# All row-tile pairs of w_sp·z2 and the product with w_out by seven block products for eight

## The chip, the cores and the metric

The kernel runs on one core of a Trainium2 chip. TensorE (PE) multiplies, VectorE (DVE), ScalarE (ACT) and GpSimd (POOL) do the element-wise work, and all transfers between DRAM and SBUF are issued in order by SyncE (SP) into one queue. The metric is the device time of one execution in microseconds, lower is better; from run to run it differs by a few tenths of a per cent.

## The reference

One block: a linear-attention half and a gMLP half, both with adaLN modulation. S = 2048 tokens, D = 512, F = 1376, Fh = F/2 = 688, float32.

```python
h = layernorm(x) * (1 + ca) + sa
x = x + ga * linear_attention(h, wqkv, wo)      # 32 heads
h = layernorm(x) * (1 + cb) + sb
z = gelu(h @ w_in)                              # (S, 1376)
z1, z2 = z[:, :688], layernorm(z[:, 688:])
g = w_sp @ z2 + b_sp[:, None]                   # (S, S) times (S, 688)
out = x + gb * ((z1 * g) @ w_out)               # (S, 688) times (688, 512)
```

## The kernel before

Tokens are cut into 16 tiles of 128 (NT = 16). Float32 accuracy comes from splitting every operand into a part rounded for fast products ("hi") and the rest ("lo"): one product is three matmuls, hi·hi, hi·lo and lo·hi (`mm3`). The hi part is an ACT copy, the lo part a DVE (at places POOL) subtraction, so that every operand costs work there before PE can use it.

The order of the work is written out by hand. `ORDER` is a list of words for the first phases (qkv, attention, x1, z), `ORDER3` for the late phase; a word is two letters and arguments (`pr1,0,3` calls `prod(1, 0, 3)`), `OPS` says which function. Each engine gets its instructions in this order, and waits for tiles with semaphores. `SLOTS` says which buffer of a pool each tile takes.

The late phase. z2 tiles (`zs` pool, hi and lo, 688 columns as two halves LO and HI of 344) stay in SBUF; their normalized values are also written to DRAM (`zd`). w_sp is loaded in pieces `raw_wsp` (512 KB). g is made in pairs of row tiles, p = 0 to 7:

- Pair 0 (row tiles 0 and 1) by plain products, `pp` (`plain`, PSUM tile Pq): 4 × 2 × 2 × 4 calls of three matmuls of 344 columns, 192 in all, with w_sp's hi and lo from `aH`, `aL`; `ce` (`q_end`) adds the bias and multiplies with z1.
- Pairs 1 to 7 by seven block products for eight, `pr` (`prod`, PSUM tiles P): the row-tile pair and a pair of source tiles form a 2×2 block matrix, the two halves of z2's columns the other side. That needs sums and differences of w_sp's blocks (`ss`, four per pair and half; hi `fh`, lo `fl` on DVE or `fg` on POOL) and of z2's (`ts` reads a pair of z2 tiles back from `zd` as e and o, `td` makes differences by four DVE subtractions, `th` and `tl` the hi and lo parts). 7 × 2 × 4 × 3 = 168 matmuls a pair, 1176 in all. `cs`, `cd` add the products up out of PSUM.

Then u = z1·g per tile (`um`), 16-bit planes of it (`up`), a transposing DMA (`ux`), a merge (`ug`), and u, now transposed, is parked in DRAM (`uq`, tile `ud`, 384 KB) and later fetched back (`ur`); `uh`, `ul` make its hi and lo parts (`ut`). `wm` (`wout_mm`) multiplies a token tile with w_out: 17 matmuls of 512 columns into tile `pout`; the last tile in two halves of 256 columns. `ot` (`out_store`) adds x1 and writes the output.

Buffers: early pools (`ws`: wk, wv and then w_in's halves; `ta`; `tb`) are closed before the late phase, and late pools (`u`, `z1`, `c1` to `c3`, `tq`) lie on their space, each tile waiting for the tiles under it.

Of the kernel before, what the change touches and what calls it, by code (L numbers as in the profile page):

```python
# [19 lines left out]
ND = 4  # L20
DIGITS = "0123456789abcdefghijklmnopqrstuvwxyz"
# [5 lines left out]
def block_kernel(ctx: ExitStack, tc: tile.TileContext, x, x_t, w_qkv, w_o, w_in, w_sp, b_sp, w_out,  # L27
# [3 lines left out]
    def pool(name, bufs, space=None, stack=None):  # L31
        if space is None:
# [6 lines left out]
    sizes2 = {"ws": ([P, 5504], 2), "ta": ([P, 512], 6), "tb": ([P, 768], 7)}  # L39
    sizes3 = {"u": ([P, 768], 2), "z1": ([P, 688], 1), "c1": ([P, 344], 1), "c2": ([P, 344], 1), "c3": ([P, 344], 1),  # L40
              "tq": ([P, 688], 24)}
# [134 lines left out]
    def silu():  # L176
        e0 = sm([P, KC], "e0")
# [167 lines left out]
    wk = sb("ws", [P, 2, KC, D], F32R, "wk")  # L345
# [338 lines left out]

    def z2_hi(t):
# [85 lines left out]
    def hx_lo(t):  # L771
# [12 lines left out]
        "lh": load_half, "aH": a_hi, "aL": a_lo, "aG": lambda t, k: a_lo(t, k, nc.gpsimd),  # L784
# [15 lines left out]
        gm5 tl10 bl7 kh6 q45 s19 k27 km8 qm7 k47 q26 ks6 lx13 k18 th13 s110 kl6 kh7 ks7 q46 q21 k28 km9 q17  # L800
# [385 lines left out]
```

## Time and profile before

| | us |
|---|---|
| median of 3 runs (range) | 617.22 (616.88 to 618.18) |
| profiled execution | 616.95 |
| its span on the core | 615.0 |
| PE busy / weight loads | 608.7 / 555.6 |
| DVE busy | 464.2 |
| ACT busy | 362.2 |
| POOL busy | 212.2 |
| granted PE clock | 1.00 |
| DMA | 105.74 MB, mean 172 GB/s |

The span is what the hardware profiler records from the first instruction to the last; the execution's own time has some 2 us around it. A row of the timeline has start, duration, engine, line, operation and tiles. A row of the groups has line, engine, operation, output<-input, shape and count, then busy us, mean ns of one, and the idle time just ahead of these instructions with what ended it. Line numbers are those of the kernel before; names have their running numbers left out.

### The profile page before, as it was taken

Reading aid. Unit: us, or ns where it says so; the run is one execution under the profiler, and the core shown is the slowest. Engines: PE = TensorE matmul, PEld = TensorE weight load, DVE = VectorE, ACT = ScalarE, POOL = GpSimd, SP = SyncE. Lnnn points to the kernel's source line nnn. Section 1 sums busy time; section 2 is a strip of 40 time slices with the busy share of each in tenths; the row PEclk is TensorE's granted clock in tenths of the full one; section 3 lists DMA queues with packets and bytes.
Section 4 is the critical chain, followed back from the end, with each engine's and each line's share of the span. In section 5 each row is a group of like instructions: output and inputs, shape, how many; then the busy total and the mean of one; then the engine's idle time right before and its main releaser. Section 6 shows DMA issues by size and latency. Waiting matters only on the chain.

```text
span 615.0 us, 9440 instructions
## 1 busy us (share of the span) xinstructions
PE 608.7 (99%) x3359; PEld 555.6 (90%) x3359; DVE 464.2 (75%) x873; ACT 362.2 (59%) x619; POOL 212.2 (34%) x180
## 2 busy tenths in 40 slices
PE   8999999999999999999999999999999999999997
PEld 6778888888889999999999999999999999998786
DVE  2889987987898787879866999966568667765643
ACT  2786765767556656565775166566565656644450
POOL 0852346536966665365320103022112121200000
PEclk9999999999999999999999999999999999999999
DMA  8352331441344866468918645564564866589973
GB/s 303 126 179 98 122 118 44 147 165 40 87 109 120 185 147 192 136 170 260 274 59 326 270 148 169 126 195 101 192 208 129 229 140 175 196 243 284 311 239 113
DMA packets 91022, 105.74 MB, mean 172 GB/s; under 512 B 57088, under 2 KB 57600, under 8 KB 90976
## 3 DMA queue, kind: packets, MB, share of 16 engines
q1 hardware_dynamic: 90976, 105.15, 56.9%
q8 instruction: 26, 0.43, 0.3%
q14 instruction: 20, 0.16, 0.1%
HBM read 66.07 MB, written 25.95 MB: 150 GB/s over the span
## 4 chain that ended last, share of the span: by engine, by line
PE 84%; DVE 7%; ACT 3%; DMA 3%; POOL 1%; issue 1%; SPq 1%; ACTq 0%; DVEq 0%; POOLq 0%
PE P L944 30%; PE z L654 13%; PE Pq L944 5%; PE z L860 2%; PE g L112 2%; PE g L110 2%; PE pout L112 2%; PE g L111 2%; PE pout L110 2%; PE pout L111 2%; PE qp L111 2%; PE qp L110 2%; PE qp L112 2%; PE kp L110 2%; PE kp L111 2%; PE kp L112 2%
## 5 line engine op out<-in xcount | busy, mean ns | idle before, releaser
L944 PE MATMUL P<-z,f 128*128 128x344 f32 x672 | 109.8, 320 | 0.0
L654 PE MATMUL z<-win,ht 128*128 128x344 f32 x672 | 107.9, 320 | 0.2 <-ACT z L659 0.2
L654 PEld LDWEIGHTS z<-win,ht 128*128 128x128 f32 x672 | 106.4, 188 | 1.3 <-ACT z L659 0.5
L944 PEld LDWEIGHTS P<-z,f 128*128 128x128 f32 x672 | 106.6, 188 | 0.0
L934 POOL TENSOR_TENSOR f<-raw_wsp,f 128x512 fp32r<-128x512 f32 x28 | 39.6, 1423 | 172.7 <-ACT f L931 150.2
L254 POOL TENSOR_TENSOR mv<-ve,mhalf 128x1 f32<-128x1 f32 x48 | 35.2, 736 | 68.3 <-DVE nm L387 34.4
L931 ACT ACTIVATE f<-raw_wsp 128x512 fp32r<-128x512 f32 x56 | 34.2, 626 | 37.2 <-PE P L944 20.3
L934 DVE TENSOR_TENSOR f<-sa,f 128x512 fp32r<-128x512 f32 x42 | 32.0, 769 | 18.5 <-ACT f L931 16.5
L931 ACT ACTIVATE f<-sa 128x512 fp32r<-128x512 f32 x42 | 25.8, 625 | 20.6 <-issue 8.4
L278 ACT COPY uca<-ucb 128x768 uint16<-128x768 uint16 x32 | 31.9, 1063 | 7.0 <-DMA ucb<-uca 6.9
L112 PE MATMUL pout<-wout,ut 128*128 128x512 f32 (+1 forms) x85 | 32.3, 380 | 0.7 <-DVE ut L1039 0.7
L110 PE MATMUL pout<-wout,ut 128*128 128x512 f32 (+1 forms) x85 | 32.5, 383 | 0.0
L111 PE MATMUL pout<-wout,ut 128*128 128x512 f32 (+1 forms) x85 | 32.2, 379 | 0.0
L1033 ACT ACTIVATE ut<-ur 128x384 fp32r<-128x384 f32 x32 | 15.6, 519 | 27.9 <-DMA ur<-ud 11.0
L944 PE MATMUL Pq<-z,wsp 128*128 128x344 f32 x192 | 31.0, 321 | 0.0
L944 PEld LDWEIGHTS Pq<-z,wsp 128*128 128x128 f32 x192 | 30.6, 188 | 0.0
L476 POOL TENSOR_TENSOR pksum<-pksum,tk 128x512 f32<-128x512 f32 x15 | 22.3, 1486 | 18.0 <-DVE tk L448 14.5
L268 ACT COPY uca<-us 128x768 uint16<-128x768 uint16 x32 | 24.9, 826 | 5.2 <-PE P L944 2.0
L583 POOL TENSOR_TENSOR prod<-pq,zrep 128x512 f32<-128x512 f32 x16 | 21.8, 1376 | 15.7 <-DVE den L591 5.0
L934 DVE TENSOR_TENSOR f<-raw_wsp,f 128x512 fp32r<-128x512 f32 x28 | 19.8, 714 | 8.3 <-ACT f L931 8.3
L112 PE MATMUL po<-m,pt 128*128 128x512 f32 x64 | 25.4, 397 | 0.1
L110 PE MATMUL po<-m,pt 128*128 128x512 f32 x64 | 25.4, 396 | 0.0
(254 smaller groups left out, 1546.4 us busy)
## 6 DMA issues: line engine op xcount, KB each, us to landing
raw_wsp<-in_w_sp SPq DMA_DIRECT2D x32, 512.0 KB, 4.5
ud<-uca SPq DMA_DIRECT2D x16, 384.0 KB, 3.5
ur<-ud SPq DMA_DIRECT2D x16, 384.0 KB, 4.7
z1d<-z SPq DMA_DIRECT2D x16, 344.0 KB, 2.5
zd<-zz SPq DMA_DIRECT2D x16, 344.0 KB, 3.2
z1r<-z1d SPq DMA_DIRECT2D x16, 344.0 KB, 4.1
xt<-in_x_t SPq DMA_DIRECT2D x16, 256.0 KB, 3.4
x<-in_x SPq DMA_DIRECT2D x16, 256.0 KB, 3.0
```

The costliest lines, as they stand in the source:

```text
L110: mm(o, a_hi, b_hi, start=first, stop=False, **kw)
L111: mm(o, a_hi, b_lo, start=False, stop=False, **kw)
L112: mm(o, a_lo, b_hi, start=False, stop=last, **kw)
L254: nc.gpsimd.tensor_tensor(mv[:, 1:2], ve, mhalf, op=OP.pow)
L268: nc.scalar.copy(pl[:, h], v[:, :, h])
L278: copy(o[:, :, h], plt[:, h * n:(h + 1) * n].rearrange("p a b -> p (a b)"))
L476: nc.gpsimd.tensor_add(pksum, pksum, PK[t])
L583: nc.gpsimd.tensor_mul(pr, PQ[t], KV["z"])
L654: mm(p[:, b, :HB], a[:, i, kc], win[h][:, j, kc, b * HB:(b + 1) * HB], start=kc == 0 and k == 0, stop=kc == KC - 1 and k == 2)
L931: nc.scalar.activation(SF[p, h, k][:, 0], s_src(p, h, k), AF.Copy)
L934: eng.tensor_sub(SF[p, h, k][:, 1], s_src(p, h, k), f(SF[p, h, k][:, 0]))
L944: mm(B[key][:, :HB], a[:, x_], b[:, y_], start=i == 1, stop=i == n)
```

## The change

1. Pair 0 of w_sp·z2 goes by the seven products too; `plain`, `q_end`, `a_hi` and `a_lo` are removed. 8 × 168 = 1344 matmuls.
2. The source tiles are paired as in `PAIRS` instead of neighbours, with w_sp's columns permuted on the host. One block difference per pair is made in place on the even tile's upper half before its hi and lo parts (`zt`, `z2_diff`): it takes the place of one of the four subtractions of `td` and of the extra hi and lo parts of form 7 (8 ACT and 8 DVE instructions of 344 columns).
3. u·w_out goes by seven products for eight per pair of tokens: the first 512 rows of w_out and its 512 columns as 2×2 blocks of 256, all matmuls of 256 columns. `op` (`o_prod`) is one block product (2 × 3 matmuls), `or` (`o_rest`) the remaining 176 rows plainly (5 matmuls, four times a pair): 62 matmuls a pair, 496 in all. Partial sums of the products are read out of PSUM between them by `oa` (`o_add`, eight a pair: six of 256 columns, two of 512), straight into x1's tile.
4. The block sums of u are made after the merge (`ua`, three DVE subtractions or sums of 256 columns a pair) and parked with u: `ud` and `ur` have 512 KB a token. The fourth is made after the return, on POOL, with hi and lo parts of its own (`uH`, `uL`). The 48-row repair of the last piece goes to POOL. w_out gets four block sums (`wa`) and nine forms.
5. The early pool `ws` becomes `w0` and `w1`, the late `tq` becomes `tq` (11) and `tr` (13) that lie on different early pools, and `ORDER`, `ORDER3` and `SLOTS` are written anew.

```diff
+PAIRS = ((0, 1), (2, 3), (4, 7), (5, 8), (6, 9), (10, 11), (12, 13), (14, 15))
...
+    sizes2 = {"w0": ([P, 5504], 1), "tb": ([P, 768], 7), "w1": ([P, 5504], 1), "ta": ([P, 512], 6)}
...
+              "tq": ([P, 688], 11), "tr": ([P, 688], 13)}
...
+    def z2_diff(t):
+        a, b = ZZ[t][:, HB:], ZZ[MATES[t]][:, HB:]
+        nc.vector.tensor_sub(a, b, a)
...
         nc.vector.tensor_sub(e0, e1, e0)
-        nc.vector.tensor_sub(e1, o1, e1)
         nc.vector.tensor_sub(o1, o1, e0)
         nc.vector.tensor_sub(o0, o0, o1)
...
+    def u_sum(p, k):
+        a, b = (UR[2 * p], UR[2 * p + 1]) if k == 4 else (u_flat(2 * p), u_flat(2 * p + 1))
+        a11, a12, a21, a22 = a[:, 256:512], a[:, 512:768], b[:, 256:512], b[:, 512:768]
+        if k == 3:
+            nc.vector.tensor_sub(a[:, :256], a11, a21)
+        elif k == 1:
+            nc.vector.tensor_add(a21, a21, a22)
+        elif k == 2:
+            nc.vector.tensor_sub(b[:, :256], a21, a11)
+        else:
+            nc.gpsimd.tensor_sub(b[:, :256], a12, b[:, :256])
...
-        UD[t] = dram.tile([P, 768], F32, tag=f"ud{t}", name=f"ud{t}")
+        UD[t] = dram.tile([P, 1024], F32, tag=f"ud{t}", name=f"ud{t}")
...
+    def o_prod(p, k):
+        b, c = {1: (0, 0), 6: (0, 0), 7: (0, 0), 4: (0, 0), 2: (1, 0), 5: (1, 1), 3: (1, 1)}[k]
+        for i in range(2):
+            v = u_form(p, k, i)
+            for x_, y_ in ((0, 0), (0, 1), (1, 0)):
+                o_mm(p, b, c, v[:, x_], WO[k][:, y_, i], i == 1 and x_ == 1)
+
+    def o_rest(p, n):
+        b, c = ((1, 0), (1, 1), (0, 0), (0, 1))[n]
+        t, h = 2 * p + n // 2, n % 2
+        v = u_rest(t, 4)
+        for x_, y_ in ((0, 0), (0, 1), (1, 0)):
+            o_mm(p, b, c, v[:, x_], WO[8][:, y_, h], False)
+        v = u_rest(t, 5)[:112, 0]
+        for y_ in range(2):
+            o_mm(p, b, c, v, WO[9][:112, y_, h], y_ == 1)
+
+    def o_add(p, n):
+        t, b, c0, c1, k = ((0, 0, 0, 256, 0), (0, 0, 256, 512, 0), (1, 1, 256, 512, 256), (1, 0, 256, 512, 0),
+                           (1, 0, 0, 256, 0), (1, 0, 256, 512, 256), (1, 0, 0, 512, 0), (0, 1, 0, 512, 0))[n]
+        o = X3[2 * p + t][:, c0:c1]
+        nc.vector.tensor_add(o, o, PO[p, b][:, k:k + c1 - c0])
+        if n > 3:
+            dma(out[(2 * p + t) * P:(2 * p + t + 1) * P, c0:c1], o)
...
-        zg12 pp0,1 zw15 zo11 zw14 aH1,2 zh13 zo13 ts1 ss1,0,2 td1 ts4 ts2 fh1,0,6 aH1,3 ts3 ts5 ts0 td4 aL1,2
+        th1,6 zh14 fh0,0,3 ss0,1,1 zo13 pr0,0,1 zo12 tl1,6 fh0,1,1 zw14 th1,4 zo14 fl0,0,3 zw15 ts3 fl0,1,1
...
-        ul12 wm10 wm11 lx12 uh13 ot9 wm12 ul13 uq15 ot10 ur15 ot11 uh14 uh15 ot12 ul14 ul15 wm13 wm14
+        oa5,6 oa6,3 uh15 op7,1 op6,3 op7,2 or6,1 ul15 or6,2 oa6,7 ua7,4 op7,5 oa7,0 oa7,2 uH7 op6,4 or7,0 uL7
```

Entry of the late phase on PE. Before, the last plain products of pair 0 (Pq, from w_sp's hi and lo parts `wsp`) and then the first block product of pair 1 (P, from forms `f`):

```order
L944 MATMUL Pq_0_3899<-z_10_3462,wsp_2_3851 128x344 x3
L944 MATMUL Pq_1_3903<-z_10_3462,wsp_2_3851 128x344 x3
L944 MATMUL Pq_0_3899<-z_11_3534,wsp_2_3851 128x344 x3
L944 MATMUL Pq_1_3903<-z_11_3534,wsp_2_3851 128x344 x3
L944 MATMUL P_3_4146<-z_1_2865,f_1_0_4120 128x344 x3
L944 MATMUL P_3_4146<-z_3_3179,f_1_0_4120 128x344 x3
L944 MATMUL P_3_4146<-z_5_3189,f_1_0_4120 128x344 x3
L944 MATMUL P_3_4146<-z_7_2859,f_1_0_4120 128x344 x3
```
Now, the end of one late z1 tile (z), the first block product of pair 0 between two of these tiles:

```order
L858 MATMUL z_12_3733<-win_1464,ht_12_3274 128x344
L858 MATMUL z_12_3734<-win_1464,ht_12_3274 128x344
L942 MATMUL P_1_3796<-z_0_2765,f_0_0_3642 128x344 x3
L942 MATMUL P_1_3796<-z_2_2779,f_0_0_3642 128x344 x3
L942 MATMUL P_1_3796<-z_4_3098,f_0_0_3642 128x344 x3
L942 MATMUL P_1_3796<-z_5_3236,f_0_0_3642 128x344 x3
L858 MATMUL z_14_3813<-win_1464,ht_14_3358 128x344
L858 MATMUL z_14_3814<-win_1464,ht_14_3358 128x344
```
The plain products that stood between the z1 tiles and the first use of a form are gone; the first form of w_sp is used while the z1 tiles still run.

The same place on DVE. Before: a pair's differences (e, o), sums and lo parts of w_sp (`sa`, `f`) and z2's lo parts (t), with the plain products still running:

```order
L934 TENSOR_TENSOR f_1_0_3874<-sa_10_3860,f_1_0_3874 128x512
L880 TENSOR_TENSOR e_3882<-e_3882 128x344
L881 TENSOR_TENSOR e_3882<-o_3883,e_3882 128x344
L882 TENSOR_TENSOR o_3883<-o_3883,e_3882 128x344
L883 TENSOR_TENSOR o_3883<-o_3883 128x344
L924 TENSOR_TENSOR sa_10_3860<-raw_wsp_0_3658,sa_10_3860 128x512
L880 TENSOR_TENSOR e_3932<-e_3932 128x344
L881 TENSOR_TENSOR e_3932<-o_3933,e_3932 128x344
L882 TENSOR_TENSOR o_3933<-o_3933,e_3932 128x344
L883 TENSOR_TENSOR o_3933<-o_3933 128x344
L934 TENSOR_TENSOR f_1_0_4039<-sa_10_3762,f_1_0_4039 128x512
L903 TENSOR_TENSOR t_2r<-o_3871,t_2r 128x344
```
Now, some 30 rows after the last lo part of z2:

```order
L878 TENSOR_TENSOR e_3931<-e_3931 128x344
L879 TENSOR_TENSOR o_3932<-o_3932,e_3931 128x344
L880 TENSOR_TENSOR o_3932<-o_3932 128x344
L929 TENSOR_TENSOR f_0_1_3984<-raw_wsp_1_3636,f_0_1_3984 128x512
L953 MEMSET us_4044 128x16
L957 SCALAR_TENSOR_TENSOR us_4044<-P_2_3950,bsp,c_0_3935 128x344
L929 TENSOR_TENSOR f_1_0_4020<-raw_wsp_0_3963,f_1_0_4020 128x512
L898 TENSOR_TENSOR t_3r<-o_3870,t_3r 128x344
L898 TENSOR_TENSOR t_4r<-o_3877,t_4r 128x344 x2
L878 TENSOR_TENSOR e_4028<-e_4028 128x344
L879 TENSOR_TENSOR o_4029<-o_4029,e_4028 128x344
L880 TENSOR_TENSOR o_4029<-o_4029 128x344
```
A pair's differences take three rows instead of four, the lo parts `f_0_1` belong to pair 0, and its first sum out of PSUM (us<-P) stands ahead of the last pairs' differences.

The end on PE. Before, the last token's last products, each column half in one row of matmuls in one bank:

```order
L110 MATMUL pout_0_6650<-wout_6126,ut_15_6604 128x256
L111 MATMUL pout_0_6650<-wout_6126,ut_15_6604 128x256
L112 MATMUL pout_0_6650<-wout_6126,ut_15_6604 128x256
L1081 MATMUL pout_0_6650<-wout_6124,ut_15_6604 128x256
L1082 MATMUL pout_0_6650<-wout_6124,ut_15_6604 128x256
L110 MATMUL pout_256_6674<-wout_6030,ut_15_6602 128x256
L111 MATMUL pout_256_6674<-wout_6030,ut_15_6602 128x256
L112 MATMUL pout_256_6674<-wout_6030,ut_15_6602 128x256
```
Now, the last pair, with the partial sums between (bank 0 and bank 1 of the pair are pout_0 and pout_1):

```order
L1127 MATMUL pout_0_6901<-wout_6101,ut_15_6897 128x256 x6
L1127 MATMUL pout_1_6914<-wout_6054,u_7_6945 128x256 x6
L1127 MATMUL pout_1_6914<-wout_6143,ut_14_6805 128x256 x3
L1127 MATMUL pout_1_6914<-wout_5904,ut_14_6805 128x256 x2
L1127 MATMUL pout_0_6901<-wout_6212,ut_14_6803 128x256 x6
L1127 MATMUL pout_0_6901<-wout_6143,ut_15_6899 128x256 x3
L1127 MATMUL pout_0_6901<-wout_5904,ut_15_6899 128x256 x2
L1127 MATMUL pout_0_6901<-wout_6143,ut_15_6899 128x256 x3
L1127 MATMUL pout_0_6901<-wout_5904,ut_15_6899 128x256 x2
L1127 MATMUL pout_0_6901<-wout_6186,ut_15_6899 128x256 x6
```
Six matmuls of a block product go into one half of a bank, and the bank changes from product to product; ahead of the last row one of the sums below has to be done.

The end on DVE. Before, one sum (x<-x,pout) per token, the last in two halves:

```order
L1039 TENSOR_TENSOR ut_14_6598<-ur_6515,ut_14_6598 128x384
L1041 TENSOR_TENSOR ut_14_6600<-ur_6515,ut_14_6600 128x256
L1042 TENSOR_TENSOR ut_14_6600<-ur_6515,ut_14_6600 48x128
L1039 TENSOR_TENSOR ut_15_6602<-ur_6594,ut_15_6602 128x384
L1041 TENSOR_TENSOR ut_15_6604<-ur_6594,ut_15_6604 128x256
L1042 TENSOR_TENSOR ut_15_6604<-ur_6594,ut_15_6604 48x128
L1086 TENSOR_TENSOR x_13_6258<-x_13_6258,pout_0_6614 128x512
L1086 TENSOR_TENSOR x_14_6047<-x_14_6047,pout_0_6632 128x512
L1086 TENSOR_TENSOR x_15_6318<-x_15_6318,pout_0_6650 128x256
L1086 TENSOR_TENSOR x_15_6318<-x_15_6318,pout_256_6674 128x256
```
Now:

```order
L1150 TENSOR_TENSOR x_11_6545<-x_11_6545,pout_0_6745 128x512
L1150 TENSOR_TENSOR x_13_6324<-x_13_6324,pout_0_6779 128x256
L1036 TENSOR_TENSOR ut_15_6897<-ur_6867,ut_15_6897 128x512
L1038 TENSOR_TENSOR ut_15_6899<-ur_6867,ut_15_6899 128x384
L1150 TENSOR_TENSOR x_12_6712<-x_12_6712,pout_1_6793 128x512
L1150 TENSOR_TENSOR x_14_6812<-x_14_6812,pout_0_6901 128x256
L1150 TENSOR_TENSOR x_15_6883<-x_15_6883,pout_1_6914 128x256
L1049 TENSOR_TENSOR u_7_6945<-ur_6867,u_7_6945 128x256
L1150 TENSOR_TENSOR x_13_6324<-x_13_6324,pout_0_6779 128x512
L1150 TENSOR_TENSOR x_14_6812<-x_14_6812,pout_0_6901 128x256
L1150 TENSOR_TENSOR x_14_6812<-x_14_6812,pout_1_6914 128x512
L1150 TENSOR_TENSOR x_15_6883<-x_15_6883,pout_0_6901 128x256 x3
```
Eight sums a pair stand there, those of 256 columns between products of the same bank, and the two lo parts of u (`ut`) and that of the late block sum (`u`) between them.

More of the change, by code (lines that the diff above doesn't have):

```diff
@@ L176, in silu @@
     def silu():
-        e0 = sm([P, KC], "e0")
+        e0 = small.tile([P, KC], F32, tag="e0", name="e0", bufs=1)
         nc.scalar.activation(e0, cT, AF.Exp, scale=-1.0)
@@ L872, in t_load @@
     def t_load(j):
-        TS[j] = [sb("s4" if j == 7 else "tq", [P, FH], F32, f"{'eo'[i]}{j}") for i in range(2)]
+        TS[j] = [sb("s4" if j == 7 else "tq" if j > 2 else "tr", [P, FH], F32, f"{'eo'[i]}{j}") for i in range(2)]
         for i in range(2):
-            dma(TS[j][i], ZD[2 * j + i])
+            dma(TS[j][i], ZD[PAIRS[j][i]])
     def t_diff(j):
@@ L937, in block_kernel @@
     BANK = {1: 0, 6: 1, 7: 2, 5: 3, 2: 4, 3: 5, 4: 6}
[L939 to L944 removed]
+    BANK0 = {1: 7, 6: 3, 7: 6, 5: 7, 2: 1, 3: 2, 4: 1}
     def prod(p, h, k):
+        if (p, k) not in B:
+            B[p, k] = bank((BANK if p else BANK0)[k], f"P{p}_{k}")
         for j in range(4):
[L948 to L953 removed]
+            a, t = SF[p, h, k][:, :, j], t_of(4 * h + j, k)
+            for x_, y_ in ((0, 0), (0, 1), (1, 0)):
+                n = COUNT[p, k] = COUNT.get((p, k), 0) + 1
+                mm(B[p, k][:, :HB], a[:, x_], t[:, y_], start=n == 1, stop=n == 24)
     C = {}
@@ L1074, in wout_mm @@
-    def wout_mm(t, c0=0, c1=D):
-        PO[t, c0] = bank((t + (c0 > 0) + 7) % 8, f"pout{t}_{c0}")
-        p = PO[t, c0][:, c0:c1]
-        for k in range(5):
-            v = UT[t, k // 3][:, :, k % 3]
-            mm3(p, v[:, 0], v[:, 1], WO[k][:, 0, c0:c1], WO[k][:, 1, c0:c1], k == 0, False)
-        v = UT[t, 1][:112, 0, 2]
-        mm(p, v, WO[5][:112, 0, c0:c1], start=False, stop=False)
-        mm(p, v, WO[5][:112, 1, c0:c1], start=False, stop=True)
-    def out_store(t, c0=0, c1=D):
-        o = X3[t][:, c0:c1]
-        nc.vector.tensor_add(o, o, PO[t, c0][:, c0:c1])
-        dma(out[t * P:(t + 1) * P, c0:c1], o)
+    PO, NPO = {}, {}
@@ new lines, in o_bank, with o_mm @@
+    def o_bank(p, b, c):
+        if (p, b) not in PO:
+            PO[p, b] = bank((2 * p + 7 + b) % 8, f"pout{p}_{b}")
+        return PO[p, b][:, 256 * c:256 * c + 256]
+    def o_mm(p, b, c, a, w, last):
+        k = p, b
+        NPO[k] = NPO.get(k, 0) + 1
+        mm(o_bank(p, b, c), a, w, start=NPO[k] == 1, stop=last, skip_group_check=True)
+    def o_prod(p, k):
[4 more added lines that the diff above has]
+                o_mm(p, b, c, v[:, x_], WO[k][:, y_, i], i == 1 and x_ == 1)
```

368 lines of the change are left out of this document (200 added, 168 removed).

## The prediction

> **What bounds the kernel now.** I read the busy shares first, then the chain that ended last, then the timeline of TensorE (PE) around the two places that the change touches.
>
> ```profile
> PE 608.7 (99%) x3359; PEld 555.6 (90%) x3359; DVE 464.2 (75%) x873; ACT 362.2 (59%) x619; POOL 212.2 (34%) x180
> ```
>
> PE is busy for 608.7 of 615.0 us: only 6.3 us are left to be won by better covering. Time goes only if PE's products go, and it comes back only where PE is made to wait. The chain says the same of the late phase (start, duration, what):
>
> ```profile
> 332.12 7.56 PE z L860 x48
> 339.68 22.90 PE Pq L944 x144
> 362.58 185.10 PE P L944 x1176
> ...
> 572.70 0.50 PE pout L112
> 576.45 0.24 PE pout L110
> ...
> 603.94 0.24 PE pout L110
> ...
> 611.96 0.42 DVE x L1086
> ```
>
> From 339.68 to 547.68 the chain is products back to back: 185.10/1176 = 0.1574 us for one of 344 columns. In the stage of u times w_out, one token of 17 products of 512 columns takes (603.94 - 576.45)/7 = 3.927 us, or 0.2310 us a product. The last token is done in products of 256 columns, which is the shape of the changed stage:
>
> ```profile
> 607.70 0.29 PE L110 MATMUL pout<-wout,ut 128*128 128x256 f32 x1
> ...
> 609.73 0.28 PE L110 MATMUL pout<-wout,ut 128*128 128x256 f32 x1
> ...
> 611.64 0.28 PE L1082 MATMUL pout<-wout,ut 112*128 112x256 f32 x1
> ```
>
> Seventeen of them start within 2.03 us: 0.1194 us each, a little over half of 0.2310. The column beside the start (0.28) is latency, not cost.
>
> **The sum.** All of it goes against the profiled execution, 616.95 us (span 615.0); the median of the runs shown is 0.27 above that.
>
> First pair of row tiles. 192 plain products go and 168 block products come, both of 344 columns: 24 x 0.1574 = -3.78 us of PE.
>
> u times w_out. Before, 15 x 17 products of 512 columns and 34 of 256: 255 x 0.2310 + 34 x 0.1194 = 62.96 us. After, 8 pairs x 62 of 256 columns: 496 x 0.1194 = 59.22 us. That is -3.74 us. It breaks even at 62.96/496 = 0.1269 us a product, 6% above the measured one, so this half hangs on the small shape keeping its pitch. [...]
>
> Entry of the late phase. Before, the plain products of the first pair needed only the hi and lo parts of w_sp and z2, and they covered VectorE (DVE) while it made the forms for the block products. Now the first pair needs those forms itself. DVE was nearly full there:
>
> ```profile
> 320.00:340.00 20.00, 20.00 (x129) 20.00 (x128) 14.57 (x31) 10.74 (x17) 1.10 (x2) 1.00 0.78 284
> 340.00:380.00 40.00, 40.00 (x254) 40.00 (x254) 38.34 (x75) 21.63 (x50) 4.77 (x3) 1.00 0.54 189
> 550.00:590.00 40.00, 39.28 (x170) 31.24 (x169) 21.25 (x46) 19.48 (x33) 0.40 (x1) 1.00 0.97 278
> 548.00:560.00 12.00, 12.00 (x53) 9.68 (x52) 6.18 (x15) 5.85 (x9) 0.52 (x1) 1.00 1.03 247
> 20.00:100.00 80.00, 79.59 (x346) 63.92 (x345) 71.11 (x131) 58.93 (x97) 38.57 (x32) 1.00 0.32 112
> ```
>
> The columns are window, length, busy us of PE, weight load, DVE, ACT, POOL, then clock, DMA share and GB/s. DVE: 38.34 of 40 (96%) from 340 to 380, 14.57 of 20 (73%) from 320 to 340, and PE lost nothing. The pitch of DVE work is read from starts that follow each other:
>
> ```profile
> 349.67 0.51 DVE L880 TENSOR_TENSOR e<-e 128x344 f32<-128x344 f32 x1
> ...
> 351.32 0.52 DVE L883 TENSOR_TENSOR o<-o 128x344 f32<-128x344 f32 x1
> 351.75 0.68 DVE L924 TENSOR_TENSOR sa<-raw_wsp,sa 128x512 f32<-128x512 f32 x1
> 352.36 1.60 DVE L880 TENSOR_TENSOR e<-e 128x344 f32<-128x344 f32 x1
> ...
> 355.53 0.68 DVE L934 TENSOR_TENSOR f<-sa,f 128x512 fp32r<-128x512 f32 x1
> 356.13 0.51 DVE L903 TENSOR_TENSOR t_2r<-o,t_2r 128x344 fp32r<-128x344 f32 x1
> 356.56 0.69 DVE L934 TENSOR_TENSOR f<-raw_wsp,f 128x512 fp32r<-128x512 f32 x1
> ...
> 364.74 1.11 DVE L903 TENSOR_TENSOR t_0r<-e,t_0r 128x344 fp32r<-128x344 f32 x1
> ```
>
> So 0.60 us for 512 columns, 0.43 for 344, 0.55 for each step of a dependent chain (349.67 to 351.32 is three), 1.54 for the three subtractions of a pair's differences. The small instructions there are these:
>
> ```profile
> L249 DVE BATCH_NORM_STATS2 bst<-zz 128x6 f32<-128x344 f32 x32 | 14.7, 502 | 3.4 <-ACT zz L665 3.4
> L253 DVE TENSOR_SCALAR ve<-mv 128x1 f32<-128x1 f32 x48 | 7.4, 154 | 1.7
> L251 DVE BATCH_NORM_AGGREGATE mv<-bst 128x2 f32<-128x12 f32 x16 | 3.3, 209 | 0.5
> L676 DVE TENSOR_SCALAR zb<-mv 128x1 f32<-128x1 f32 x16 | 3.1, 205 | 1.5 <-POOL mv L254 1.5
> ```
>
> Before the first pair's block products are through, DVE has to do, by the order of the change: statistics of the last four z2 tiles, 8 + 4 + 4 instructions (8 x 0.50 + 4 x 0.21 + 4 x 0.15 = 5.5, some 5.1 us with their overlap) and four offsets (0.6); 26 of 344 columns (11.2); eight difference chains (12.3); four lo parts of z2 of 688 columns (0.80 each by columns, 3.2); 21 of 512 columns, sums and lo parts of w_sp (12.6); three sums out of PSUM (1.4). That is 46.4 us. PE covers about 50.0 us of it: the late z1 products, 96 x 0.1574 = 15.1; the pair's 168 products, 26.4; the next pair's first 12, 1.9; 0.5 of another product; and some 6 us of PE before the last z1 tile, from the moment the first of these z2 tiles is there.
>
> Five POOL instructions lie in the same stretch, and the trace shows what one costs DVE:
>
> ```profile
> 351.87 1.72 POOL L934 TENSOR_TENSOR f<-raw_wsp,f 128x512 fp32r<-128x512 f32 x1 [27.16 <-ACT f L931]
> 364.08 1.40 POOL L934 TENSOR_TENSOR f<-raw_wsp,f 128x512 fp32r<-128x512 f32 x1 [10.50 <-ACT f L931]
> 370.94 1.65 POOL L934 TENSOR_TENSOR f<-raw_wsp,f 128x512 fp32r<-128x512 f32 x1 [5.46 <-ACT f L931]
> ```
>
> The DVE instructions started at 352.36 and 364.74, within the first two of them, took 1.60 and 1.11 instead of 0.51: 0.6 to 1.1 us each, so 3.0 to 5.5 for five, 4.3 in the middle. At DVE's 96% the stretch takes 46.4/0.96 = 48.3 us without that (nothing late) and 50.7/0.96 = 52.8 with it (2.8 late). I take +1.5, the middle; below nothing is excluded since PE has no idle time there to win. [...]
>
> u times w_out, its waits. Partial sums are read from PSUM between products, and PE may not go on in that bank until DVE has read. Such a read costs what DVE's last row shows:
>
> ```profile
> L1086 DVE TENSOR_TENSOR x<-x,pout 128x256 f32<-128x256 f32 x2 | 0.8, 422 | 2.9 <-PE pout L1082 2.9
> L1086 DVE TENSOR_TENSOR x<-x,pout 128x512 f32<-128x512 f32 x15 | 10.1, 686 | 6.2 <-PE pout L1082 6.0
> L1039 DVE TENSOR_TENSOR ut<-ur,ut 128x384 fp32r<-128x384 f32 x16 | 8.9, 556 | 16.9 <-ACT ut L1033 16.9
> L1041 DVE TENSOR_TENSOR ut<-ur,ut 128x256 fp32r<-128x256 f32 x16 | 6.7, 421 | 6.1 <-ACT ut L1033 6.0
> ```
>
> 0.28 (end of the product) + 0.42 = 0.70 us where nothing lies between. In the changed order another bank's products (0.36 to 0.72 us for 3 to 6) stand between nearly everywhere; the first pair, with no pair ahead of it, has one bare read (0.7), the last about 0.2, and I put 0.1 on the rest: +1.0. From below it is 0; from above one bare read for each pair, 8 x 0.70 = 5.6. DVE itself keeps up: a pair needs two lo parts of 512 columns and two of 384, one of 256, six sums of 256 and two of 512, at durations 2 x 0.69 + 2 x 0.56 + 7 x 0.42 + 2 x 0.69 = 6.8 us, while PE takes 62 x 0.1194 = 7.4. If a POOL instruction there (one of 256 columns a pair, two small ones) blocks it for 0.6, it is just even.
>
> What I cost at nothing. The block sums of u before parking (24 DVE instructions of 256 columns, 0.42 each, 10 us) lie under 185 us of products, where DVE also loses 8 steps of the differences and the lo parts of the eight forms that are now made once in z2; the w_out sums (4) likewise. The extra parking, 128 KB out and 128 KB back for 16 tokens, 4.2 MB, is spread over that stage apart from its end (below). The new order of the first two phases: PE idles 0.41 us in 20 to 100 us, so at best half a microsecond is there to win; a misplaced wait could lose 1 to 2; I take 0. The tail, a sum of 256 columns and its store, is the same.
>
> Sum: 616.95 - 3.78 - 3.74 + 1.5 + 1.0 = 611.9; on the median's scale **612.2 us**. The terms' own range is 609.7 to 614.7.
>
> **Rivals.**
>
> All hidden. Both waits are covered and only products count: 616.95 - 7.52 + 0.27 = 609.7; with the 0.7 that PE lost at 572.70 and the 0.4 in 20 to 100 won too, 608.6. For it: PE lost nothing under a DVE at 96%. Against: the entry is tighter than that by count.
>
> DVE late at the entry. If DVE runs there at the 73% of 320 to 340, because it waits for ACT's hi parts and for the z2 tiles that come back from DRAM, 46.4/0.73 = 63.6 us, 13.6 late: 612.2 - 1.5 + 13.6 = 624.3. It eats the whole gain at 46.4/s - 50.0 = 6.5 us, s = 0.82. Against: before, DVE ran at 96% as soon as it had the loads.
>
> Transfers bound the last stage. All DMAs go through one queue:
>
> ```profile
> ud<-uca SPq DMA_DIRECT2D x16, 384.0 KB, 3.5
> ur<-ud SPq DMA_DIRECT2D x16, 384.0 KB, 4.7
> x<-x1d SPq DMA_DIRECT2D x16, 256.0 KB, 4.0
> out<-x SPq DMA_DIRECT2D x15, 256.0 KB, 3.2
> ```
>
> With ud and ur at 512 KB, from the third token's return to the last's the queue carries 14 returns (7.34 MB), three parkings (1.57), nine x3 (2.36), ten outputs (2.62), one z1 (0.35) and two transposes (0.79): 15.0 MB. The last must have landed some 53.2 us after the first starts (51.2 of products ahead of its use and 2 of head start). At the 278 GB/s of 550 to 590, with its DMA share of 0.97, that is 54.0 us, 0.8 late, which the +1.0 holds. At the 247 of 548 to 560 it is 60.7, 7.5 late: 612.2 - 1.0 + 7.5 = 618.7, slower than before; the gain is gone below 254 GB/s. Against it: 278 is a mean over 40 us, with stretches of other work in it, and the queue runs ahead of PE wherever it is faster.
>
> The small products cost more in this stream than in the last token, where 17 of them follow each other with one operand kept hot. The change then doesn't save what it says. If they went at the 0.1574 of the 344 columns, the stage would take 78.1 us, 15.1 longer than before: 612.2 + 3.74 + 15.1 = 631. It turns the whole change slower above (62.96 + 3.78 - 2.5)/496 = 0.1295 us.
>
> **How the numbers follow.** A difference of 0.2% (1.23 us) is about what a measurement of this kernel can tell from none. Chances: forecast 0.62; all hidden 0.11; DVE late 0.15 (0.06 still faster, 0.04 even, 0.05 slower); transfers 0.07 (0.01, 0.02, 0.04); dear small products 0.05, slower. So faster 0.62 + 0.11 + 0.06 + 0.01 = 0.80, same 0.06, slower 0.14. The range that leaves out 2 in 10 runs from 608.6, the floor, to 617.0, half-way into the late-entry cases.
>
> **What would show it.** Right: PE's products back to back through the first pair, its idle time grown by 1 to 3 us in all; the pout groups at about 59 us for 496; the sums of the last stage waiting for PE and not PE for them. Wrong: a gap on PE at the first pair's products behind DVE's t or f (entry), gaps behind ur (transfers), pout products starting more than 0.127 us apart without a wait (price), or idle time on PE in the first 300 us, which would be the new order and which I put at nothing.

## The result: slower by 1.3%, and where it shows in the profile after

The changed kernel took 625.69 us (median of 5 runs, 624.86 to 627.25) and the kernel before 617.85 beside it: ratio 1.0132, 95% interval 1.0114 to 1.0150. The forecast was 612.2 with a range of 608.6 to 617.0. The profiled execution took 624.86 us, its span 623.1 us, 8.1 longer than before.

The page of the changed kernel, the row that answers to the first one shown (busy us, share of the span, instructions):

```profile
PE 606.1 (97%) x3542; PEld 561.9 (90%) x3542; DVE 497.7 (80%) x933; ACT 370.7 (59%) x629; POOL 236.8 (38%) x208
```

PE's busy time fell by 2.6 us only, and its idle time grew from 6.3 to 17.0. Two tables say where. The first is of marks that I read from PE's timeline:

| us from the span's start | before | after | lost in the stage that ends here |
|---|---|---|---|
| first product of k and v (pkv) | 150.49 | 151.19 | +0.70 |
| first transposition of the second half's h (tph) | 174.34 | 181.71 | +6.67 |
| first product of the late phase | 316.80 | 324.39 | +0.22 |
| first product with w_out | 547.51 | 554.47 | -0.63 |
| end of the last one | 611.92 | 619.91 | +1.03 |

The second is the head of the list of what PE waited for in the changed kernel (sum, times, longest):

```profile
PE pm L117 <- DVE m L135: 4.0, 2, 2.5
PE pout L1127 <- DVE x L1150: 4.0, 6, 1.0
PE P L942 <- POOL f L929: 1.1, 1, 1.1
PE warm L179 <- POOL ones L127: 1.0, 1, 1.0
PE P L942 <- ACT z L864: 0.9, 1, 0.9
PE z L858 <- ACT mod L247: 0.7, 1, 0.7
```

**The seam.** The largest loss lies in a stage that the prediction put at nothing: between the attention sums (kv) and the output projection, where four products `mm0` to `mm3` (tile pm) multiply kv with wo and their hi and lo parts (`me`, tile m) are made for the products po. The timelines of PE, before and then after (start, duration, engine, line, operation):

```profile
160.29 0.39 PE L112 MATMUL pm<-wog,kvh 128*128 128x512 f32 x1
160.51 0.40 PE L110 MATMUL qp<-wq,ht 128*128 128x512 f32 x1
...
164.07 0.47 PE L110 MATMUL po<-m,pt 128*128 128x512 f32 x1
```

```profile
162.39 0.40 PE L119 MATMUL pm<-wog,kvh 128*128 128x512 f32 x1
165.26 0.50 PE L117 MATMUL pm<-wog,kvh 128*128 128x512 f32 x1 [2.47 <-DVE m L135]
...
168.23 0.79 PE L117 MATMUL pm<-wog,kvh 128*128 128x512 f32 x1 [1.58 <-DVE m L135]
...
170.39 0.78 PE L117 MATMUL po<-m,pt 128*128 128x512 f32 x1
170.96 0.63 PE L118 MATMUL po<-m,pt 128*128 128x512 f32 x1
171.39 0.63 PE L119 MATMUL po<-m,pt 128*128 128x512 f32 x1
```

Before, all four pm products ran through, and 12 query products (qp) covered DVE until po began. In the new order `mm1` and `mm3` stand behind `me0` and `me2`. Two pm products share one PSUM tile of two halves, and the second was not written before DVE had read the first: `mm1` and `mm3` waited 2.47 and 1.58 us for it. On DVE that reading stands behind other work the first time (pt at 163.93) and waits for ACT's hi part of m the second time:

```profile
163.93 0.68 DVE L135 TENSOR_TENSOR pt<-tpp,pt 128x512 fp32r<-128x512 f32 x1
164.52 0.68 DVE L135 TENSOR_TENSOR m<-pm,m 128x512 fp32r<-128x512 f32 x1
166.89 1.29 DVE L135 TENSOR_TENSOR m<-pm,m 128x512 fp32r<-128x512 f32 x2 [1.68 <-ACT m L134]
```

The idle time has a second price. The windows of ten us, before and then after (the third column from the end is the granted clock):

```profile
160.00:170.00 10.00, 10.00 (x48) 8.09 (x48) 8.52 (x17) 7.70 (x15) 9.79 (x8) 1.00 0.29 87
170.00:180.00 10.00, 9.90 (x53) 8.48 (x52) 9.19 (x19) 3.95 (x9) 7.60 (x7) 1.00 0.41 116
```

```profile
160.00:170.00 10.00, 5.95 (x25) 4.26 (x24) 5.97 (x10) 3.71 (x9) 9.08 (x7) 0.84 0.27 89
170.00:180.00 10.00, 10.00 (x39) 8.13 (x38) 6.81 (x14) 4.41 (x8) 4.84 (x5) 0.82 0.29 84
```

The two pauses make 4.05 us of idle time within six, and in the second of them the clock fell: windows of one us give 0.91 from 166 to 167, 0.50 in each from 167 to 173, and 1.00 again from 174. The last pm products and the first po products started 0.43 us apart (170.96, 171.39) instead of 0.23 until about 173.7. The 15 products started from 168.23 on (three pm, four tpp, eight po) took 5.59 us to the start at 173.82; by the starts in the same trace at a clock of 1.00 (0.80 for three pm from 165.26, 0.36 for four tpp from 157.99, 0.33 and 7 x 0.23 for eight products behind them) they would take 3.1, so the clock cost some 2.5 us (an estimate). Together with the idle time that is 6.5 of the 6.7 us lost in this stage. The pitch agrees with the granted clock: 0.23/0.43 is 0.53, beside 0.50. How long a pause it takes is not shown.

**The end.** On PE, a stretch of the w_out stage in which nothing waits, then the last products of the last pair; below, the sums on DVE that these wait for:

```profile
597.07 7.64 PE L1127 MATMUL pout<-wout,ut 128*128 128x256 f32 x62 [0.60 <-DVE x L1150]
604.55 0.85 PE L1127 MATMUL pout<-wout,u 128*128 128x256 f32 x6
...
618.33 1.58 PE L1127 MATMUL pout<-wout,ut 128*128 128x256 f32 x11 [0.97 <-DVE x L1150]
```

```profile
616.09 0.69 DVE L1150 TENSOR_TENSOR x<-x,pout 128x512 f32<-128x512 f32 x1 [0.90 <-PE pout L1127]
617.40 0.88 DVE L1150 TENSOR_TENSOR x<-x,pout 128x256 f32<-128x256 f32 x2 [0.62 <-PE pout L1127]
```

62 products in 604.55 - 597.07 = 7.48 us are 0.1206 us each, so the small products kept their price. But the stage took 65.44 us for 59.22 of products: 6.2 over, of which 4.0 are the six waits for partial sums. Before, it took 64.41 us for 62.96 of products, 1.45 over, so what the change added is 4.8. Four of the six waits (0.51, 0.51, 0.60 and 0.97) stand at reads with no matmul in between. The other two, 0.41 and 1.02 in the first pair, have five or six; ahead of the reads behind the longer one DVE makes lo parts of w_out (556.83 to 558.65).

**The entry.** PE lost 0.75 us there behind `mB5` (the modulation's last product, read out of PSUM by ACT), and 0.86 us behind a gelu on ACT that stood still for a store:

```profile
343.44 0.42 SPq L866 DMA_DIRECT2D z1d<-z  x1
```

```profile
348.58 0.81 ACT L864 ACTIVATE z<-z 128x344 f32<-128x344 f32 x2 [1.83 <-DMA z1d<-z]
```

```profile
349.09 2.14 PE L942 MATMUL P<-z,f 128*128 128x344 f32 x12 [0.86 <-ACT z L864]
```

The last four z1 tiles share one buffer (`st`, number 0) in the new `SLOTS`, so the gelu of token 15 has to wait until token 14's tile is in DRAM, and that store (343.44) stands on SP's queue behind the loads e and o of z2 (342.58, 342.95); in the chain it took 5.06 us until it had landed.

### The profile page after: what moved, and what is told of

It is laid out like the page before. It is cut to its first block, busy times and chain, and to the rows that moved or that the text cites. A ratio compares the mean times of both kernels' runs of the same rounds, so it can differ in the third digit from the quotient of the medians.

```text
span 623.1 us, 9978 instructions
## 1 busy us (share of the span) xinstructions
PE 606.1 (97%) x3542; PEld 561.9 (90%) x3542; DVE 497.7 (80%) x933; ACT 370.7 (59%) x629; POOL 236.8 (38%) x208
## 4 chain that ended last, share of the span: by engine, by line
PE 84%; DMA 5%; DVE 5%; ACT 2%; POOL 2%; issue 1%; SPq 1%; ACTq 0%; POOLq 0%; DVEq 0%
PE P L942 30%; PE z L661 14%; PE pout L1127 9%; PE z L858 2%; PE qp L117 2%; PE qp L118 2%; PE g L119 2%; PE qp L119 2%; PE g L118 2%; PE g L117 2%; PE kp L119 2%; PE kp L117 2%; PE kp L118 2%; PE po L117 2%; PE po L119 2%; PE po L118 2%
## 5 line engine op out<-in xcount | busy, mean ns | idle before, releaser
L942 PE MATMUL P<-z,f 128*128 128x344 f32 x768 | 125.8, 320 | 0.9 <-ACT z L864 0.9
L942 PEld LDWEIGHTS P<-z,f 128*128 128x128 f32 x768 | 121.8, 188 | 1.2 <-ACT z L864 1.1
L929 POOL TENSOR_TENSOR f<-raw_wsp,f 128x512 fp32r<-128x512 f32 x32 | 46.8, 1468 | 170.3 <-ACT f L926 114.6
L1127 PE MATMUL pout<-wout,ut 128*128 128x256 f32 (+1 forms) x448 | 56.9, 284 | 4.1 <-DVE x L1150 4.0
L1127 PEld LDWEIGHTS pout<-wout,ut 128*128 128x128 f32 (+1 forms) x448 | 54.6, 189 | 5.6 <-DVE x L1150 2.9
L926 ACT ACTIVATE f<-raw_wsp 128x512 fp32r<-128x512 f32 x64 | 39.2, 626 | 29.4 <-PE P L942 20.3
L1150 DVE TENSOR_TENSOR x<-x,pout 128x256 f32<-128x256 f32 (+1 forms) x49 | 23.3, 498 | 15.3 <-PE pout L1127 15.1
L1030 ACT ACTIVATE ut<-ur 128x512 fp32r<-128x512 f32 x32 | 18.9, 625 | 22.9 <-DMA ur<-ud 14.9
L1039 POOL TENSOR_TENSOR ut<-ur,ut 48x128 fp32r<-48x128 f32 x16 | 11.4, 714 | 43.7 <-ACT ut L1030 43.7
L117 PE MATMUL po<-m,pt 128*128 128x512 f32 x64 | 26.1, 408 | 0.0
L119 PE MATMUL po<-m,pt 128*128 128x512 f32 x64 | 25.8, 402 | 0.0
L118 PE MATMUL po<-m,pt 128*128 128x512 f32 x64 | 25.7, 402 | 0.0
```

What stands on the lines that cost most here:

```text
L117: mm(o, a_hi, b_hi, start=first, stop=False, **kw)
L118: mm(o, a_hi, b_lo, start=False, stop=False, **kw)
L119: mm(o, a_lo, b_hi, start=False, stop=last, **kw)
L926: nc.scalar.activation(SF[p, h, k][:, 0], s_src(p, h, k), AF.Copy)
L929: eng.tensor_sub(SF[p, h, k][:, 1], s_src(p, h, k), f(SF[p, h, k][:, 0]))
L942: mm(B[p, k][:, :HB], a[:, x_], t[:, y_], start=n == 1, stop=n == 24)
```

## The experiments

Each kernel was compared with the kernel before on its own chip, and the ratio is against that. Kernels that are set against each other below shared a chip unless it is said; across chips, only ratios are compared.

**The seam alone.** All four pm products ahead of the evacuations, nothing else.

```diff
-... ae2 mm0 mm2 me0 lW1,2 wh1,0 wl1,0 d14 mm1 at1 me1 me2 mm3 wl1,1 ...
+... ae2 mm0 mm2 mm1 mm3 me0 lW1,2 wh1,0 wl1,0 d14 at1 me1 me2 wl1,1 ...
```

> The changed kernel (625.7 us) with two words moved: the third and fourth product group of the attention's second matrix (mm1, mm3 into tile pm) ahead of the first evacuation (me0) instead of behind it. Theory 'shared tile': PE waits 4 us at 162 to 170 because mm1 and mm3 write the other half of a PSUM tile whose first half is still being read, and the clock drops after it. Then the idle time there falls to 1 to 2 us, the granted clock stays at 1.00, and the time is 620 to 621.5. Rival 'DVE queue': PE would wait for DVE's lo parts of m anyway, behind tq and pt. Then less than 1.5 us is won: 624 to 625.5.

Measured: 623.01 us (621.48 to 624.74), ratio 1.0089 (1.0061 to 1.0118). Its windows:

```profile
160.00:170.00 10.00, 9.54 (x44) 7.11 (x43) 7.85 (x14) 5.62 (x11) 9.53 (x7) 1.00 0.27 89
170.00:180.00 10.00, 10.00 (x51) 8.32 (x50) 8.68 (x18) 4.76 (x10) 9.33 (x8) 1.00 0.38 114
```

The clock's drop and all but half a microsecond of the idle time are gone with two words moved, as the theory of the shared tile has it. From pkv to tph it takes 24.68 us (30.52 in the changed kernel, 23.85 before). Of these 5.8 us, 4.9 are still there at the start of the late phase and 3.4 in the span; what uses up the rest in the late phase is not shown. So the time missed the theory's 620 to 621.5: by the ratios, 1.0089 here and 1.0132 for the changed kernel on another chip, some 2.7 us were won.

**The seam with before's cover.** As mm_ahead, with two more words moved (`qm14`, `q114`) so that query products stand between pm and po.

```diff
-... at0 qm14 ae0 q114 ae2 mm0 mm2 mm1 mm3 me0 ...
+... at0 ae0 ae2 mm0 mm2 mm1 mm3 qm14 q114 me0 ...
```

> As the run before, and q's last 12 products and their tq (qm14, q114) behind these groups, where the kernel before has such products too. 'Shared tile': the rest of the wait is covered, 618.5 to 619.5, and nothing is lost between 150 and 185 us against the kernel before. 'DVE queue': this run wins what the first didn't, 619 to 621. Rival 'spread': the new order loses its 7 us in many places and only 2 or 3 come back, 622 or more.

Measured: 624.72 us (622.70 to 626.37), ratio 1.0125 (1.0096 to 1.0155). That is in the range of the rival 'spread'. By the medians it is 1.7 worse than mm_ahead, though the two intervals overlap. The products that were moved had covered something themselves, as this kernel's list of waits shows:

```profile
PE pm L117 <- ACT kvh L134: 1.5, 1, 1.5
```

**No partial reads.** As mm_ahead_cover, but the sums that read PSUM between the products of a pair are left out, with the terms that they add to the output.

```diff
 def o_add(p, n):
+    if n < 4:
+        return
```

> As mm_ahead_cover, without the four sums per pair that read partial products out of PSUM (n below 4 in o_add; those terms are missing from the output). Theory 'bare reads': PE waits in the last stage for sums that have no other product beside them: 4 to 5.5 us less than mm_ahead_cover, 613.5 to 615, and the stage of 496 products takes 59.5 to 60.5 us. Rival 'price or transfers': the products of 256 columns or the returning u set the stage's time, and less than 1 us is won: 618 or more.

Measured: 619.22 us (616.04 to 623.03, 10 runs), ratio 1.0039 (1.0013 to 1.0064); the w_out stage took 61.0 us in place of 65.5. So the reads cost about 4.5 us, and without them the stage is within 1.8 of its products' 59.22. The gain on mm_ahead_cover is 5.5 by the medians, as 'bare reads' expected; the time itself is above the expected 613.5 to 615, because mm_ahead_cover was slower than assumed. This kernel also spares DVE 32 sums, so by itself it doesn't tell the waits at the banks from a DVE that is full; the next one keeps the sums.

**Reads covered.** As mm_ahead_cover, all reads kept, the words of the last stage moved so that at least 5 matmuls (in most places 11 or more) stand between the last write ahead of a read and the next write to its bank, and one lo part of w_out (`os7`) stands behind the first pair's reads. Extracts of the moved words:

```diff
-... op3,7 uL3 oa3,3 or3,3 lx10 or4,3 oa4,0 op4,6 ... ul10 op3,3 op4,3 ...
+... oa4,0 ua4,4 ... op3,7 uL3 op3,3 oa3,3 or3,3 lx10 or4,3 op4,6 ... ul10 op4,3 ...
-... op7,5 oa7,0 oa7,2 uH7 op6,4 or7,0 uL7 op7,6 op7,3 or7,1 oa6,6 oa7,1 op7,7 or7,3 oa7,7 oa7,3 oa7,5 or7,2
+... op7,5 oa7,0 oa7,2 uH7 or7,3 op7,6 oa7,1 uL7 op6,4 or7,0 op7,7 oa6,6 op7,3 oa7,3 or7,1 oa7,5 or7,2 oa7,7
```

> As mm_ahead_cover, with words of the last stage moved so that every read of a partial sum has at least 5 products of the other bank or pair beside it (five reads had none: oa3,3 oa4,0 oa5,0 oa7,3 oa7,5), and one lo part of w_out behind the first pair's reads. 'Bare reads': 2 to 3.2 us less than mm_ahead_cover, 615.5 to 617. Rival 'DVE full': the waits come from a DVE that is busy there, less than 0.7 us is won.

Measured: 622.13 us (619.91 to 622.62), ratio 1.0067 (1.0041 to 1.0094): 2.6 us less than mm_ahead_cover, which is what 'bare reads' said of the difference and more than the 0.7 of 'DVE full'; the time is again above its range with mm_ahead_cover's. The row of its list of waits, 2.0 us in place of 4.0:

```profile
PE pout L1127 <- DVE x L1150: 2.0, 2, 1.3
```

**The old order of the first phases.** Two kernels take `ORDER` and `SLOTS` of the kernel before for the first two phases (and pairs of source tiles that fit them), so that the seam is the old one; the in-place difference of z2 (`zt`) stands right behind the store of the tile in the first, and in the second 14 words behind it where the order allows. Of the two kernels with the reads covered, the first also has the load `ts4` behind a store at the entry.

```diff
-PAIRS = ((0, 1), (2, 3), (4, 7), (5, 8), (6, 9), (10, 11), (12, 13), (14, 15))
+PAIRS = ((0, 2), (4, 1), (5, 7), (3, 6), (9, 8), (11, 10), (12, 13), (14, 15))
```

> The changed kernel with the order and the buffers of the first two phases as before the change (the attention, x1 and z), the new late phase unchanged; source tiles are paired (0,2) (4,1) (5,7) (3,6) (9,8) (11,10), as that order allows. Theory 'order': the first two phases are what makes the change slower, 7 to 7.6 us of it: 617.5 to 619, even with the kernel before or a little slower. Rival 'late phase': the products saved there are paid back by DVE and transfers more than the profile of one run shows, and 621 or more stays.

> As the run before, with the words of the last stage moved as in reads_covered, and the loads ts4 behind the store of z1's tile 14. 'Order' and 'bare reads' together: 2 to 3.5 us less than the run before, 614.5 to 616.5, faster than the kernel before by 0.1 to 0.4%. If the late phase is the rival's, 619 or more.

> As old_first_phases (645.9 us, in which DVE stood 23 us behind the stores that a block difference of z2 has to wait for), with these differences 14 words behind their stores where the order allows it, and the buffers of z and z1 given out anew. 'Order': the first two phases come back to within 1 to 3 us of before, 618 to 621. Rival 'differences': the eight differences in z2's own tiles don't fit under the old order's z phase wherever they stand, since they keep two z2 tiles and a store alive; 626 or more.

> As old_first_phases_2 with the last stage's words of reads_covered: 2 to 2.6 us less than it, 615.5 to 619; only below 615.8 would it be faster than the kernel before.

Measured: 645.91 (ratio 1.0486, 1.0461 to 1.0511) and, with the reads covered, 640.47 (1.0391, 1.0371 to 1.0411); 633.11 (1.0265, 1.0242 to 1.0289) and 628.92 (1.0197, 1.0170 to 1.0223). All four are above their theories' ranges; the second kernel's time is in that of the rival 'differences'. The seam is as short as before (tph at 174.2 and 174.6), but what follows loses far more than it gains: the late phase starts at 336.5 and 326.2 (316.8 before), and at its entry PE waits another 4.0 us for a form from DVE in each. DVE's largest wait in old_first_phases is the difference that may not overwrite a tile before its store has landed:

```profile
DVE zz L694 <- DMA zd<-zz: 23.0, 5, 5.5
```

In the second this wait is down to 1.8 us, once, and its z products still lose. So the old order and the new differences didn't go together in either of the two placings; whether a third would do stays open. Covering the reads gave 5.4 (with `ts4` moved) and 4.2 us in these two pairs, more than the 2.6 beside mm_ahead_cover.

**The entry.** As mm_ahead, with the last mod evacuation (`mB5`) ahead of z's product of token 15 (`z115`), and one load of z2 behind the store that the gelu waits for.

```diff
-... zh10 z115 g213 g214 g215 mB5 ...
+... zh10 mB5 z115 g213 g214 g215 ...
-... th0,4 ts4 fl0,0,7 th0,6 pr0,1,1 th2,4 pr0,0,7 zg14 ...
+... th0,4 fl0,0,7 th0,6 pr0,1,1 th2,4 pr0,0,7 zg14 ts4 ...
```

> As mm_ahead (623.0 us), with two edits at the entry of the late phase: the modulation's product mB5 ahead of the last early z1 tile, and the loads ts4 behind the store of z1's tile 14. Theory 'buffer': PE's two waits there (0.7 on mod, 0.7 to 0.9 on z) come from the place of mB5 and from one buffer that all four late z1 tiles share, whose store stands behind two loads of 344 KB in the queue; 1 to 1.6 us less, 621.4 to 622. Rival 'DVE late', as predicted: DVE is what the entry lacks, and the waits only move to f and t: less than 0.4 us less.

> As seam_entry, with the last stage's words of reads_covered. If the three causes are separate they add: 2 to 3 us less than seam_entry, 618.5 to 620. If one only hides another, less than 1 us.

Measured: 623.94 us (1.0115, 1.0097 to 1.0133), and with the reads covered 621.20 (1.0072, 1.0052 to 1.0092), 2.7 us less. mm_ahead ran on another chip with 1.0089, so the entry's words show no gain: the waits moved, as the rival said, to DVE's forms (1.74 at 330.48) and to a z product next to the moved word (1.32 at 316.82). From the list of seam_entry:

```profile
PE P L941 <- DVE f L928: 2.3, 2, 1.7
PE z L661 <- ACT zz L672: 1.3, 1, 1.3
```

**Both causes mended, nothing else.** The words of mm_ahead and those of reads_covered, beside the changed kernel on the same chip.

> The changed kernel once more, beside the next ones: 624.9 to 626.5. Whatever mm_ahead and its variants won is read against this one.

> mm_ahead with the last stage's words of reads_covered and nothing else. If the seam (2.5 to 4 us) and the bare reads (2 to 2.6 us) add: 619.5 to 621.5, the best of the new order, still slower than before (617). If not separate: 622 or more.

Measured: changed_again 627.14 us (1.0169, 1.0143 to 1.0195), 0.6 above what was expected, seam_and_reads 619.18 (616.22 to 621.12, 9 runs; 1.0026, 1.0007 to 1.0045). Of the 10.1 us that changed_again is above its kernel before, the two orders take away 8.0. What is left at the entry is the gelu's wait, in the list of seam_and_reads, and the chain shows the store behind it (start, duration, what):

```profile
PE P L942 <- ACT z L864: 2.2, 1, 2.2
```

```profile
339.12 6.42 DMA z1d<-z
345.63 0.47 ACT z L864
346.14 81.42 PE P L942 x516
```

**Own buffers.** As seam_and_reads, but the z1 tiles of tokens 13 and 15 lie in buffers of `tr` and `tq`; no word of the order is moved (the expectation's words on the order are mistaken). The second kernel also moves `mB5` one word ahead and swaps two products of pair 4 (`pr4,0,4` and `pr4,0,5`).

```diff
-        z = sb("st", [P, 2, HB], F32, f"z1_{t}")
+        z = sb("tr" if t == 13 else "tq" if t == 15 else "st", [P, 2, HB], F32, f"z1_{t}")
```

> As seam_and_reads (619.18), but two of the four late difference tiles of z1 are stored and read from a second st buffer instead of all four sharing buffer 0, at the places of the order where they come two sooner and later. Theory (the entry's wait is the shared buffer: z15's gelu waits for the store that reads it, and the product behind it waits 2.2 us): that wait goes, 617.0 to 618.4, and the wait of P on z in the profile falls below 0.5 us. Rival (DVE is late at the entry anyway): the wait moves to a flaw or a mod evacuation on DVE, 618.7 to 619.7. Rival (the store is late because of the loads that stand ahead of it on SP's queue): the wait stays at about 2, 619 to 620.

> As own_st_buffers, with the last mod block's evacuation moved one z product earlier and the two first products of the fourth late pair swapped, so that the flaw difference has one product more of cover. Theory: another 0.5 to 1.2 us less than own_st_buffers, 616.2 to 617.5, that is at or just below the kernel before (617.1): what is left of the change is then the products saved (7.5) less the waits that remain. Rival (DVE's lateness, so that a wait only moves): within 0.5 of own_st_buffers.

Measured: own_st_buffers 616.67 us (613.90 to 618.46, 10 runs) against 616.90 of before, ratio 0.9987 (0.9972 to 1.0003), where seam_and_reads on another chip had 1.0026 (1.0007 to 1.0045); own_st_buffers_entry 620.60 (617.80 to 621.47, 10 runs), ratio 1.0043 (1.0028 to 1.0058), a miss of both its theory and its rival. The gelu's wait is gone from the first list, and a short one for DVE's forms is there:

```profile
PE P L941 <- DVE f L928: 0.8, 2, 0.5
```

The chain there shows what is late next: a load of z2 and the differences made from it.

```profile
340.65 7.52 DMA o<-zd
348.26 0.53 DVE o L878
...
350.28 0.70 DVE f L928
351.02 13.53 PE P L941 x84
```

The second kernel lost nothing at the entry, but 2.7 us in pair 4, where own_st_buffers has no wait. Two rows of its timeline:

```profile
455.69 0.72 PE L941 MATMUL P<-t_0r,f 128*128 128x344 f32 x3 [1.49 <-DVE us L956]
463.11 1.84 PE L941 MATMUL P<-z,f 128*128 128x344 f32 x10 [1.18 <-POOL f L928]
```

A wait of 1.3 us at g, ahead of all the edited words, is in this profile and not in that of own_st_buffers. The two edits were not run apart; the waits of pair 4 stand where the swap is. own_st_buffers is the best version found. It can't be told from the kernel before.

## Why the prediction was wrong, step by step

- **"The new order of the first two phases ... I take 0"** (at worst 1 to 2): it measured +7.6 us up to the late phase, 6.7 of them at the seam. This is the largest failed step. The bound was drawn from the idle time that there was to win (0.41 us), and the loss was guessed. The order of the change already showed `mm1` behind `me0` on one PSUM tile; I hadn't followed the moved words of this stage. The last sentence on what would show it wrong, idle time on PE in the first 300 us, is what came.
- **"u times w_out, its waits: +1.0"** measured +4.8: the stage became 1.03 us longer where the products alone would have made it 3.74 shorter. That "another bank's products ... stand between nearly everywhere" was said without a count. Counted word by word in the changed order, five reads have no matmul between (`oa3,3`, `oa4,0`, `oa5,0`, and `oa7,3` with `oa7,5` at one place), and PE waited at these four places for 2.6 us. The price of a bare read, 0.70, was about right (0.51 to 0.97). In the first pair the one bare read of 0.7 became two waits, 1.4 us, though five or six matmuls stand there. The 4.8 is within the upper end of 5.6.
- **First pair, -3.78, and the entry, +1.5.** From the start of the late phase to the first product with w_out the gain was 0.63, so 3.1 were given back: 0.75 + 0.86 + 1.1 = 2.7 of it in three waits. The entry's share, 1.6, is the size forecast, but not its cause: the waits ended with ACT (mod, and the gelu behind the store), not with DVE. DVE's lateness is real behind it: it appears where those waits are taken away (1.74 at the entry of seam_entry, 0.54 in own_st_buffers). The third wait, 1.1 for a form from POOL in pair 4, stood in no term.
- **The sum and its range.** By stages the account closes: 616.95 - 3.78 - 3.74 + 7.59 + 3.15 + 4.77 = 624.94, against 624.86 in the profiled execution. The "terms' own range" up to 614.7 was too narrow by the prediction's own bounds: 609.7 + 2.8 (entry) + 5.6 (reads) is 618.1.
- **POOL beside DVE, "0.6 to 1.1 us each".** The two rows stand, but not as a price for each POOL instruction, though this hardly moves the sum. The DVE instruction of 352.36 ends at 353.96, 0.37 us after POOL's (353.59); that of 364.74 ends at 365.85, also 0.37 after (365.48). A third, 371.48 with 1.49 us, ends 0.38 after POOL's 372.59. So in these three rows DVE's instruction ended 0.37 to 0.38 us after POOL's, and how long it took (1.60, 1.11 and 1.49 us instead of 0.51) goes with where in POOL's 1.72, 1.40 and 1.65 us it started: 0.49, 0.66 and 0.54 us into them. What makes it longer is not shown.
- **"Small products at 0.1194"** held: 0.1206. The rival of dear products, at 0.1574, is refuted. The operand "kept hot" in the last token was a guess: there too each product has a weight load of its own (85 of each in L110 of the kernel before).
- **"Transfers bound the last stage"** was not seen: no wait of PE behind ud or ur is among those listed for the stage. In mm_ahead one wait of 1.02, in the first pair, is put down to ACT's `ut`, which had itself waited 0.46 for ur; in the changed kernel the wait of 1.02 at this place is put down to the sums.
- **"DVE late at the entry"** with its 13.6 us did not occur. The time came close to its 624.3 by another cause, which lends that rival nothing. In the two kernels with the old order of the first phases a wait of this kind is there, 4.0 us.
- **"All hidden, 609.7"**: own_st_buffers, with the seam, the reads and the gelu's buffer mended, still stands at 616.67. In its profiled run, the slowest of the ten, it keeps 2.0 us of reads, 0.8 at DVE's forms, 0.7 behind mod, and pkv starts at 152.6 where before it starts at 150.5; 1.4 of these 2.1 are a wait for a load at the very start, which the changed kernel's list doesn't have. Whether an order exists in which the 7.5 us of products come through stays open.

The causes that runs have shown are the seam (its waits and its clock with mm_ahead; with the reads, 8.0 us on one chip), the reads (four pairs of kernels with and without them covered, 2.6 to 5.4 us, and no_partial_reads) and the buffer (own_st_buffers; that comparison goes over two chips, by the ratios 1.0026 and 0.9987). What the seam alone is worth in time is known only across chips. That the clock's drop goes with the pauses is read from the windows, not tried apart from the idle time.

## What to carry to other kernels

Where a change rewrites a hand-made order, the stages that it "only" moves need the same count as the stage that it is for: for each product, which tile it writes, who has to read that tile first, and how many instructions stand ahead of that reader. Here 7.5 us of saved products on an engine that was 99% busy went into waits of 0.4 to 2.5 us, and each wait that was taken away showed the next one. If a partial sum is read from PSUM in mid-stream, count the matmuls between it and the next write to that bank; none between cost 0.5 to 1.0 us here, and five or six did not always suffice where DVE had other work ahead of the read.

## What was not expected of the hardware

A pause of PE can cost more than its length, and the same pause doesn't always cost the same. In the changed kernel's seam, pauses of 2.47 and 1.58 us were followed by a granted clock of 0.50 up to about 173.7, some 2.5 us on top (the estimate above). In changed_again, with pauses of 2.46 and 1.57 us at the same place, the products started some 0.43 us apart only up to 172.86, and from 173.11 on some 0.23. There a single pause of 2.16 us at the entry (ending at 350.56) was followed by twelve products of 344 columns that took 3.45 us from start to next start. In seam_and_reads, behind a pause of 2.24 us at the same place (ending at 346.14), the same twelve took 2.00, and the clock of 340 to 350 was 1.00. What decides between them is not shown.

The runs of the changed kernel's variants also spread more than those of the kernel before: 613.90 to 618.46 for own_st_buffers over 10 runs, 616.44 to 619.88 for the kernel before over 21 beside it, all but the highest of them at or below 618.30. The cause of that is open too.
